# First transforms with regrouped channels and two-bank PSUM tiles, and a wider second inverse transform, in a convolution and two-expert-layer kernel

## The chip, the cores and the metric

The kernel runs on 1 core of one Trainium2 chip. The metric is the device time of one execution in microseconds (us). Before the change the median of 3 runs is 1278.2 us (1269.12 to 1280.97). A measurement of this kernel can tell about 1% from no change.

## The reference, cut to what matters

Three layers follow one another. `x` is (4, 5696, 128), `h` is (5696, 128); every number is fp32.

```python
# 1: long convolution along the sequence, channel by channel
Xf = np.fft.rfft(x, n=2*S, axis=1); Hf = np.fft.rfft(h, n=2*S, axis=0)
x = np.fft.irfft(Xf * Hf[None], n=2*S, axis=1)[:, :S].reshape(B*S, D)
# 2: soft mixture of experts over 32 slots
logits = x @ phi                        # (22784, 32)
d = softmax of logits over tokens;      slot_input = d.T @ x
slot_out[e] = relu(slot_input[e] @ w1[e]) @ w2[e]
x = (softmax of logits over slots) @ slot_out
# 3: top-1 routed mixture of 8 experts
e = argmax(x @ w_gate + modality_bias[modality_id]);  out = gate * (relu(x @ w1[e]) @ w2[e])
```

The change touches how layer 1 is transformed and how the slot logits and slot inputs of layer 2 are made. Layer 3 (more than half of the time) is not touched.

## The kernel before

The convolution is done with a transform written as two matmul steps. The sequence of 5696 is split as 89 x 64 (`N1`, `N2`). The first step is a transform of length 89 over the partitions, the second one of length 64 with the twiddle factors in its matrix `G`. There are five sequences in turn: `h`, then the four batches of `x`.

**Stage 1 of each sequence (`st1`, `columns`).** The sequence lies in `xr` as 89 partitions by (channel half, s, 64 channels). For one channel of each half the stationary operand (the weights that TensorE, PE in the profile, loads before a matmul) is `x[:, :, d+i]`: 128 columns, each 64 floats (256 bytes) from the next. The moving operand is `fw1`, 180 columns of cosines and sines. A PSUM tile `psa` of one bank takes two such matmuls. (An fp32 matmul is two instructions in the trace, each with its weight load, so a sequence has 64 matmuls and 128 instructions.) A tile is emptied into `A` by four copies of 64 lanes x 180 elements: two on ScalarE (ACT), lanes 0 to 63 (L124), two on VectorE (DVE), lanes 64 to 127 (L126). The framework orders any two instructions of different engines that touch the same PSUM bank, so the DVE copies of a tile wait for its ACT copies. Four tiles are in rotation (`psa`, bufs=4), a tag that `psy` and `psl2` share later.

**Steps of each sequence (`X`, `YT`, `PH`, `YL`).** 23 steps of four frequencies. `X` multiplies `A` (weights 2 floats apart) with `G`; for `x` DVE multiplies the result with the spectrum of `h` into U and V (L192, L193), GpSimd (POOL) adds and subtracts them into Y (L195, L196). Three steps later `YT` turns Y and ACT copies it out (L206) for a store, `PH` projects it on phi (`psl`, L216, copied by ACT, L220), and `YL` turns the projection (`psl2`, copied by ACT, L235). During the steps SyncE's queue (SP) loads the next sequence, in eight pieces of two DMAs. The last steps of a sequence run among the first of the next. Small jobs (`w2split_jobs`) that split a weight matrix, one ACT cast (L300) and one DVE subtraction (L301) each, are taken one after each group of four `psa` tiles.

**`slot_logits`.** `psi` (L368): the first inverse step on the projected spectrum, 128 lanes in and 89 out, copied into `A2` by ACT and DVE in turn. `psb` (L390): the second inverse step, 16 groups of 16 instructions, contracting over 89 lanes, with weights from `c_iv2` (`Bt`, four tiles in rotation, two DMAs each, loaded three groups ahead). Each `psb` group is copied by ACT into `L` (L405), then by DVE (L397), which also takes maxima (L399). After the last group a chain of small DVE and PE instructions makes the column maximum `cm`.

**`slot_inputs`.** `less` subtracts `cm` (DVE, then POOL), `weights` takes the exponential on ACT (L503), and `columns` transforms the weights `L` with the same `fw1` into `AW` (`psw`, contiguous weights, 32 tiles of one bank, 4 in rotation); now and then the DVE takes one of ACT's copies (`swap`). Transform, dot with the stored spectra and so on follow.

Everything here is in `tc.manual_schedule()`: each engine runs its instructions in the order of the program, and SP its DMAs. `yr.load()` issues the load of one 512 KB piece of the stored spectra into a ring of 19 slots that lie in `xr`, `ring`, `a2` and `Lf`. PE runs short warm-up matmuls (`keep_warm`) at a few places.

Of the kernel before, what the change touches and what calls it, by code (L numbers as in the profile page):

```python
# [12 lines left out]
F32 = mybir.dt.float32  # L13
# [8 lines left out]
B, S, D = 4, 5696, 128  # L22
# [32 lines left out]
def shape_constants():  # L55
# [54 lines left out]
NB = (N1 + 3) // 4  # L110
NPAIR = (N1 + 1) // 2


def columns(nc, ps, xs, fw1, n, put, swap=False, view=lambda v: v):

    m = len(xs)
    f = fw1.rearrange("p (r k) -> p r k", r=2)[:, :, :n]
    for i, x in enumerate(xs):
        nc.tensor.matmul(ps[:, i], x, f, start=True, stop=True)  # L119
    for j in range(2):  # L120
        for r in range(2):
            o, v = put(r, j), view(ps[64 * j:64 * j + 64, :m, r])
            if j == 0 and not (swap and r):
                nc.scalar.copy(o, v)  # L124
            else:
                nc.vector.tensor_copy(o, v)  # L126


def conv_spectra(nc, tc, I, R, P, jobs, xr, ahead):

    G, ident, phi, fw1 = P["G"], P["ident"], P["phi"], P["fw1"]
    with tc.tile_pool(name="p1", bufs=1) as sp, tc.tile_pool(name="p1p", bufs=2, space=PS) as pp:
        H = sp.tile([128, N1, 128], F32, name="H")
        A = sp.tile([128, NPAIR, D, 2], F32, name="A")
        seqs = [("h", 0)] + [("x", b) for b in range(B)]
        xt = xr.rearrange("p (h s d) -> p h s d", h=2, d=64)[:N1]
        nc.gpsimd.memset(xr[64:], 0.0)

        def load(q, c):

            if q < len(seqs):
                src = I["x"][seqs[q][1]].rearrange("(p s) (h d) -> p h s d", s=N2, h=2)
                h, s = divmod(c, 4)
                dma89(nc.sync, xt[:, h, 16 * s:16 * s + 16], src[:, h, 16 * s:16 * s + 16])

        def load_h():

            src = I["h"].rearrange("(p s) d -> p s d", s=N2)
            t = A.rearrange("p k d e -> p (k d e)")[:N1, :N2 * D].rearrange("p (s d) -> p s d", d=D)
            for c in range(0, N2, 16):  # L150
                dma89(nc.sync, t[:, c:c + 16], src[:, c:c + 16])
            for c in range(0, N2, 16):
                for h in range(2):
                    o, v = xt[:, h, c:c + 16], t[:, c:c + 16, 64 * h:64 * h + 64]
                    if h == 0:
                        nc.scalar.copy(o, v)  # L156
                    else:
                        nc.vector.tensor_copy(o, v)

        def st1(c):  # L160

            for d in range(8 * c, 8 * c + 8, 2):
                ps = pp.tile([128, 2, 2, 2 * NPAIR], F32, name="psa", tag="psa", bufs=4)
                x = xr.rearrange("p (m d) -> p m d", d=64)
                columns(nc, ps, [x[:, :, d + i] for i in range(2)], fw1, 2 * NPAIR,
                        lambda r, j: A[64 * r:64 * r + 64, :, 64 * j + d:64 * j + d + 2].rearrange("p k d e -> p d k e"),
                        view=lambda v: v.rearrange("p i (k e) -> p i k e", e=2))

        load_h()
        keep_warm(nc, pp, P["ones"], NWARM, tag="psa", bufs=4)  # L170

        class Seq:
# [4 lines left out]
            def X(self, i):  # L177
# [4 lines left out]
                if self.kind == "h":  # L182
# [4 lines left out]
                    return  # L187
                U = sp.tile([128, 4, 2, 64], F32, name="U", tag="U", bufs=2)
                V = sp.tile([128, 4, 2, 64], F32, name="V", tag="V", bufs=2)
# [3 lines left out]
                nc.vector.tensor_tensor(V[:, :n], psv[:, :n], h[:, :, 1:2, :].to_broadcast([128, n, 2, 64]), op=ALU.mult)  # L193
                y = sp.tile([128, 4, 2, 64], F32, name="Y", tag="Y", bufs=LAG + 3)
                nc.gpsimd.tensor_tensor(y[:, :n, 0], U[:, :n, 0], V[:, :n, 1], op=ALU.subtract)  # L195
# [3 lines left out]
            def YT(self, i):  # L199
                n = nk4(i)  # L200
                y = self.Y[i]
                ps = pp.tile([128, 4, 128], F32, name="psy", tag="psa", bufs=4)
                for m in range(n):
                    turned(nc, ps[:, m, :], y[:, m].rearrange("p r c -> p (r c)"), ident)
                yt = sp.tile([128, 4, 128], F32, name="yt", tag="yt", bufs=3)
                nc.scalar.copy(yt[:, :n], ps[:, :n])  # L206
                nc.sync.dma_start(R["yt"][:, self.b, 4 * i:4 * i + n, :], yt[:, :n])

            def PH(self, g):

                ps = pp.tile([128, 2, 128], F32, name="psl", tag="psl", bufs=1)
                n = min(8, N1 - 8 * g)
# [12 lines left out]
            def YL(self, g):  # L225
# [4 lines left out]
                o = self.o[:, 8 * (g % 2):8 * (g % 2) + n]  # L230
                ps = pp.tile([128, 2, 128], F32, name="psl2", tag="psa", bufs=4)
                if n == 8:
# [28 lines left out]
        for q in range(len(seqs)):  # L261
            z = Seq(q)
            for c in range(8):
                st1(c)
                if q > 0 and jobs and c < 7:
                    jobs.pop(0)(sp)
                if q == 0 and c < 6:
                    P["loadG"](c)
            for i in range(NB):
                for _ in range(2 if i == 0 else 1):  # L270
                    if tail:
                        tail.pop(0)()
                z.step(i)
                if q > 0 and i == 18 and jobs:
                    jobs.pop(0)(sp)
                if i % 2 == 0 and i < 16:
                    load(q + 1, i // 2)
# [62 lines left out]
def slot_logits(nc, tc, I, R, P, a2, xr, yr, Lf):  # L340

    ident, ones, iv1 = P["ident"], P["ones"], P["iv1"]
    L = Lf.rearrange("p (j s) -> p j s", s=N2)
    A2 = a2[:N1].rearrange("p (x j) -> p x j", x=128)
    yls = [t[:, YLW * i:YLW * i + YLW] for t in (xr, Lf) for i in range(2)]
    with tc.tile_pool(name="p2", bufs=1, reuse_waits="tile") as sp, tc.tile_pool(name="p2p", bufs=3, space=PS, reuse_waits="tile") as pp:
        Bt = {}
        BC = 4

        def load_yl(b):  # L350
            nc.sync.dma_start(yls[b], R["ylt"][b].rearrange("p k s -> p (k s)"))

        def load_B(c):
            if c < N2 // BC:
                t = sp.tile([N1, BC, 2, N1], F32, name="Bt", tag="Bt", bufs=4)
                dma89(nc.sync, t, I["c_iv2"][:, BC * c:BC * c + BC])
                Bt[c] = t
        nc.gpsimd.memset(Lf[64:, 2 * YLW:], 0.0)
        load_yl(2)
        load_yl(3)  # L360
        for _ in range(4):
            yr.load()
        for b in range(B):
            yl = yls[b].rearrange("p (k s) -> p k s", s=NS)
            for s in range(0, NS, 4):
                ps = pp.tile([N1, 4, 128], F32, name="psi", tag="a")
                for j in range(4):
                    nc.tensor.matmul(ps[:, j], yl[:, :, s + j], iv1, start=True, stop=True)  # L368
                o = A2[:, :, b * NS + s:b * NS + s + 4].rearrange("p x j -> p j x")
                if s % 8 == 0:  # L370
                    nc.scalar.copy(o, ps)
                else:
                    nc.vector.tensor_copy(o, ps)
            for _ in range((2, 4, 0, 0)[b]):
                yr.load()
            if b < 3:
                load_B(b)
        SC = 8
# [3 lines left out]
        for s in range(0, N2, 4):  # L382
            c = s // SC
            if s % SC == 0:
                st = sp.tile([N1, B, SC, NS], F32, name="lst", tag="lst", bufs=2)
            ps = pp.tile([N1, 4, B, NS], F32, name="psb", tag="a")
# [25 lines left out]
        keep_warm(nc, pp, ones, W1, tag="w", bufs=1)  # L412
        pt = pp.tile([NS, N1], F32, name="pt", tag="a")
        turned(nc, pt, m1, ident[:N1, :N1])
# [5 lines left out]
        keep_warm(nc, pp, ones, W2, tag="w", bufs=1)  # L420
        pb = pp.tile([N1, NS], F32, name="pb", tag="a")
        nc.tensor.matmul(pb, ones[:NS, :N1], dg, start=True, stop=True)
# [55 lines left out]
def slot_inputs(nc, tc, I, R, P, a2, yr, L, cm, c, prefetch, cT):  # L478

    G, fw1 = P["G"], P["fw1"]  # L480
    with tc.tile_pool(name="p3p", bufs=2, space=PS, reuse_waits="tile") as pp:
# [30 lines left out]
        weights(8, JC)  # L512
        for j in range(0, 128, 4):
            ps = pp.tile([128, 2, 2, N1 + 1], F32, name="psw", tag="a", bufs=4)
            columns(nc, ps, [L[:, j + i:j + i + 2].rearrange("p j s -> p (j s)") for i in (0, 2)], fw1, N1 + 1,
                    lambda r, i: AW[64 * r:64 * r + 64, :, j + i:j + i + 3:2].rearrange("p k j e -> p j k e"), j % 16 == 4,
                    view=lambda v: v.rearrange("p i (k e) -> p i k e", e=2))
            if j % 8 == 0 and j + JC < 128:
                weights(j + JC, j + JC + 8)
            if j % JC == JC - 4:  # L520
                yr.load()
# [22 lines left out]
        for i in range(NB + 1):  # L544
# [6 lines left out]
            if i >= 12:  # L551
                cT.make(pp, tag="a", bufs=4)
        prefetch()
# [884 lines left out]
```

## Time and profile before

| what | us |
|---|---|
| median of 3 runs | 1278.2 |
| the profiled execution, its own time | 1284.36 |
| its span, first to last instruction | 1282.5 |
| PE busy in the span | 985.3 |
| DVE busy | 680.9 |
| ACT busy | 607.8 |
| POOL busy | 527.0 |

[...] The convolution runs to about 360 us, `slot_logits` to about 454 us, `slot_inputs` to about 544 us; the rest is the experts, the routing and the routed experts. A line of the trace names the engine, the line of the kernel, the operation, the tiles (written tile, arrow, read tiles) and shapes; "idle before" is the engine's idle time ahead of the instruction and what ended it.

### The profile page before, as it was taken

The page shows a single profiled execution, that of the slowest core. Times are in us where ns is not written, and L with a number is a line of the kernel's source. Part 1 is how long each engine was busy: PE and PEld are TensorE (multiplying, and loading weights), DVE is VectorE, ACT ScalarE, POOL GpSimd, SP SyncE. Part 2 cuts the span into 40 slices and gives each one's busy share as a digit, 9 for nine tenths or more (in the row PEclk, how much of TensorE's full clock was granted, in tenths as well). Part 3 has the DMA queues.
Part 4 walks back from the last instruction along what each step waited for, and adds up shares of the span by engine and source line. Part 5 has one row for each costly group of instructions (what it writes and reads, how often), then busy time and mean ns, then how long its engine had stood idle before and what let it go on. Part 6 is the DMA issues. An engine that isn't in the chain of part 4 may idle for free.

```text
span 1282.5 us, 23978 instructions
## 1 busy us (share of the span) xinstructions
PE 985.3 (77%) x7670; PEld 907.4 (71%) x7670; DVE 680.9 (53%) x1421; ACT 607.8 (47%) x1519; POOL 527.0 (41%) x603
## 2 busy tenths in 40 slices
PE   7999999999999988983229723540018999999996
PEld 7998988889899966843129623540017999999996
DVE  3577777868734589353008512430005666666664
ACT  4464655657444272221008511420006777777775
POOL 2006345270720045126740357267663444444443
PEclk8999999999999599986559856775558999999999
DMA  9538576583785468974210000001011111111112
GB/s 281 78 73 202 169 186 204 155 249 121 245 294 145 113 221 258 359 240 135 68 45 14 13 13 15 10 21 34 28 33 37 38 38 39 38 38 40 36 40 76
DMA packets 151600, 142.45 MB, mean 111 GB/s; under 512 B 72156, under 2 KB 126876, under 8 KB 150348
## 3 DMA queue, kind: packets, MB, share of 16 engines
q1 hardware_dynamic: 139752, 125.04, 33.6%
q0 software_dynamic: 11456, 14.79, 3.9%
q8 instruction: 64, 1.05, 0.4%
q10 hardware_dynamic: 264, 1.05, 0.2%
q14 instruction: 64, 0.52, 0.1%
HBM read 218.45 MB, written 57.77 MB: 215 GB/s over the span
## 4 chain that ended last, share of the span: by engine, by line
PE 66%; another core or an unknown queue 12%; issue 9%; DVE 7%; ACT 4%; DMA 2%; POOL 0%; SPq 0%; ACTq 0%; POOLq 0%; DVEq 0%
PE psa L119 11%; PE ph L1091 9%; PE psx L181 9%; PE acc L1105 5%; PE acc L1104 5%; PE acc L1106 5%; PE psb L390 3%; PE psi L368 3%; PE psy L93 3%; PE pso L93 3%; PE psl L216 2%; ACT yT L1110 2%; DVE A L126 2%; PE psS L540 1%
## 5 line engine op out<-in xcount | busy, mean ns | idle before, releaser
L1094 DVE SCALAR_TENSOR_TENSOR hl<-ph,hh 128x512 fp32r<-128x512 f32 x360 | 247.9, 691 | 249.1 <-ACT hh L1093 125.0
L1129 POOL DMA_INDIRECT out<-y,rt x180 | 174.9, 972 | 222.0 <-ACT y L1118 175.8
L1093 ACT ACTIVATE hh<-ph 128x512 fp32r<-128x512 f32 x360 | 216.1, 602 | 99.8 <-PE ph L1091 48.5
L1091 PE MATMUL ph<-x,wm 128*128 128x256 f32 x720 | 164.1, 312 | 104.5 <-ACT x L1082 65.0
L1001 POOL DMA_INDIRECT s_rec<-rec,posi x178 | 173.3, 974 | 134.1 <-issue 53.6
L1105 PE MATMUL acc<-hl,wo 128*128 128x256 f32 x720 | 208.0, 289 | 5.0 <-issue 5.0
L1104 PE MATMUL acc<-hh,wo 128*128 128x256 f32 x720 | 208.2, 289 | 1.5 <-issue 1.5
L1106 PE MATMUL acc<-hh,wo 128*128 128x256 f32 x720 | 207.8, 289 | 1.8 <-issue 1.8
L1091 PEld LDWEIGHTS ph<-x,wm 128*128 128x128 f32 x720 | 114.5, 199 | 106.9 <-ACT x L1082 66.9
L195 POOL TENSOR_TENSOR Y<-U,V 128x256 f32<-128x256 f32 (+1 forms) x92 | 65.4, 711 | 222.5 <-DVE V L193 222.0
L119 PE MATMUL psa<-fw,xr 128*128 128x180 f32 x640 | 143.0, 386 | 6.8 <-ACT xr L156 6.8
L119 PEld LDWEIGHTS psa<-fw,xr 128*128 128x128 f32 x640 | 142.0, 313 | 8.2 <-issue 8.2
L1105 PEld LDWEIGHTS acc<-hl,wo 128*128 128x128 f32 x720 | 142.5, 198 | 5.3 <-issue 5.1
L1106 PEld LDWEIGHTS acc<-hh,wo 128*128 128x128 f32 x720 | 142.4, 198 | 1.7 <-issue 1.7
L1104 PEld LDWEIGHTS acc<-hh,wo 128*128 128x128 f32 x720 | 142.3, 198 | 1.2 <-issue 1.2
L181 PE MATMUL psx<-G,A 128*128 128x128 f32 x890 | 125.9, 289 | 3.0 <-DVE A L126 1.5
L181 PEld LDWEIGHTS psx<-G,A 128*128 128x128 f32 x890 | 113.3, 199 | 20.2 <-DVE U L192 12.4
L126 DVE COPY A<-psa 64x180 f32<-64x180 f32 x320 | 111.6, 349 | 28.4 <-ACT A L124 20.0
L124 ACT COPY A<-psa 64x180 f32<-64x180 f32 x320 | 98.2, 307 | 37.0 <-PE psa L119 34.5
L93 PE MATMUL pso<-ident,yT 128*128 128x128 f32 x180 | 39.9, 305 | 72.7 <-issue 58.6
L206 ACT COPY yt<-psy 128x512 f32<-128x512 f32 (+1 forms) x92 | 52.6, 572 | 83.1 <-PE psy L93 65.4
L1082 ACT CAST x<-pst 128x256 fp32r<-128x256 f32 x90 | 33.6, 373 | 115.1 <-PE pst L93 59.0
(197 smaller groups left out, 1420.5 us busy)
## 6 DMA issues: line engine op xcount, KB each, us to landing
wo<-s_wsc SPq DMA_DIRECT2D x90, 1024.0 KB
wm<-s_mwsc SPq DMA_DIRECT2D x180, 256.0 KB
s_yt<-yt SPq DMA_DIRECT2D x88, 256.0 KB
xr<-x SPq DMA_DIRECT2D x32, 320.0 KB
xr<-s_yt SPq DMA_DIRECT2D x20, 512.0 KB
s_wsc<-ws SPq DMA_DIRECT2D x32, 256.0 KB
L<-s_yt SPq DMA_DIRECT2D x16, 512.0 KB
s_ylt<-ylt SPq DMA_DIRECT2D x20, 256.0 KB
```

The lines of the kernel that those rows point to most:

```text
L93: nc.tensor.transpose(out, in_, ident)
L119: nc.tensor.matmul(ps[:, i], x, f, start=True, stop=True)
L126: nc.vector.tensor_copy(o, v)
L181: nc.tensor.matmul(ps[:, m, :], A[:, 2 * i + m // 2, :, m % 2], G[:, 4 * i + m, :], start=True, stop=True)
L1001: i = nc.gpsimd.indirect_dma_start(R["rec"], bass.IndirectOffsetOnAxis(ap=posi[:, g:g + 1], axis=0), rec[:, g, :], None, bounds_check=SPAR ...
L1091: nc.tensor.matmul(ps[:, TM * j:TM * j + TM], wm[k % 3][:, 128 * f:128 * f + 128], x[k], start=True, stop=True)
L1093: nc.scalar.activation(o, ps, AF.Relu)
L1094: nc.vector.scalar_tensor_tensor(hl[:, 2 * q:2 * q + 2].rearrange("p j t -> p (j t)"), ps, 0.0, o.bitcast(F32), op0=ALU.max, op1=ALU.subtract)
L1104: nc.tensor.matmul(acc[k], wh, hh[:, f], start=(f == 0), stop=False)
L1105: nc.tensor.matmul(acc[k], wh, hl[:, f], start=False, stop=False)
L1106: nc.tensor.matmul(acc[k], wl, hh[:, f], start=False, stop=(f == 7))
L1129: i = nc.gpsimd.indirect_dma_start(out, bass.IndirectOffsetOnAxis(ap=r[:, j, NS + 1:RW].bitcast(I32), axis=0), y[:, j, :], None, bounds_ch ...
```

## The change

- The sequence is loaded into `xr` as (s, 128 channels), in four pieces of two DMAs, `h` too (which came through `A` before, copied into `xr` by ACT and DVE).
- `spread(c)` copies four channel pairs at a time, 89 lanes x 512 elements, into one of three small tiles `xs`, where the weights of a matmul are 2 floats (8 bytes) apart. POOL does it three tiles ahead; for the first three tiles of a batch ACT does it in the steps 17, 19 and 21 of the sequence before.
- `columns` now takes a PSUM tile of two banks with four matmuls, two tiles in rotation. The four copies are of 64 lanes x 360 elements, and the ACT copies and the DVE copies of one tile are declared free of each other. `psw` uses the same function, in 16 tiles.
- `psl` and `psl2` become two halves of one PSUM bank that is allocated once; U and Y become one tile in 5 buffers.
- `psb` contracts over 128 lanes: `c_iv2` has zero rows, `A2` gets zeros by four POOL memsets (lanes 96 to 127) and by the `psi` copies (lanes 89 to 95, from three PSUM tiles that DVE clears first). `Bt` chunks 0 to 3 are loaded at the start into four tiles, 4 to 11 into `xr` after the second batch of `psi`, 12 to 15 as the tiles come free, with one DMA each. Six `yr.load()` move from the `psi` stage to the groups 12 to 14 of `psb`.

```diff
+NXS = 3
+def columns(nc, tc, pp, xs, fw1, put, swap=False, **k):
+    ps = pp.tile([128, 4, 256], F32, **k)
+    pv = ps[:, :, :4 * NPAIR].rearrange("p i (r k e) -> p r i k e", r=2, e=2)
     for i, x in enumerate(xs):
-        nc.tensor.matmul(ps[:, i], x, f, start=True, stop=True)
+        nc.tensor.matmul(ps[:, i, :4 * NPAIR], x, fw1, start=True, stop=True)
     for j in range(2):
         for r in range(2):
-            o, v = put(r, j), view(ps[64 * j:64 * j + 64, :m, r])
+            o, v = put(r, j), pv[64 * j:64 * j + 64, r]
             if j == 0 and not (swap and r):
-                nc.scalar.copy(o, v)
+                i = nc.scalar.copy(o, v)
+                tc.declare_no_dep(i.ins, group="half1", ...)
+                tc.add_to_no_dep_group("half0", i.ins)
...
+        xs = [sp.tile([128, 2, 128, 2], F32, name=f"xs{i}") for i in range(NXS)]
+        xv = xr.rearrange("p (s h q e) -> p q h s e", h=2, q=32, e=2)[:N1]
+        def spread(c, eng=None):
+            o, v = xs[c % NXS][:N1].rearrange("p q (h s) e -> p q h s e", h=2), xv[:, 2 * c:2 * c + 2]
+            if eng is nc.scalar:
+                nc.scalar.copy(o, v)
+            else:
+                nc.gpsimd.tensor_copy(o, v)
...
-            for c in range(8):
+            if q == 0:
+                for c in range(NXS):
+                    spread(c)
+            for c in range(16):
                 st1(c)
+                if c + NXS < 16:
+                    spread(c + NXS)
-                if q > 0 and jobs and c < 7:
+                if q > 0 and jobs and c % 2 and c < 14:
                     jobs.pop(0)(sp)
...
+        for x in range(0, 16 * F, 4 * F):
+            nc.gpsimd.memset(a2[96:, x:x + 4 * F], 0.0)
+        pst = [pp.tile([128, 4, 128], F32, name=f"psi{i}", tag=f"a{i}", bufs=1) for i in range(3)]
+        for t in pst:
+            nc.vector.memset(t[64:], 0.0)
...
-            load_B(s // BC + 3)
+            if s // BC < NBT:
+                load_B(s // BC + N2 // BC - NBT)
+            if s // BC >= N2 // BC - NBT and s // BC < N2 // BC - NBT + 3:
+                yr.load()
+                yr.load()
```

## Rows read from the trace of the kernel before

**Rows 1.** Page, part 4: chain that ended last, shares by line.
```profile
PE psa L119 11%; PE ph L1091 9%; PE psx L181 9%; PE acc L1105 5%; PE acc L1104 5%; PE acc L1106 5%; PE psb L390 3%; PE psi L368 3%; PE psy L93 3%; PE pso L93 3%; PE psl L216 2%; ACT yT L1110 2%; DVE A L126 2%; PE psS L540 1%
```
**Rows 2.** Windows: length, busy (count) of PE, PEld, DVE, ACT, POOL; clock; DMA, GB/s.
```profile
19.10:48.60 29.50, 29.43 (x128) 29.23 (x128) 21.14 (x61) 19.02 (x62) 0.00 (x0) 0.93 0.41 167
60.00:72.00 12.00, 12.00 (x104) 12.00 (x104) 4.47 (x7) 3.53 (x7) 0.00 (x0) 1.00 0.77 118
142.10:170.50 28.40, 28.40 (x134) 28.39 (x131) 23.49 (x68) 21.73 (x71) 1.69 (x4) 1.00 0.37 112
360.50:400.40 39.90, 39.90 (x257) 39.79 (x256) 15.59 (x16) 17.09 (x19) 2.17 (x1) 1.00 0.77 247
401.60:410.60 9.00, 8.94 (x80) 8.75 (x80) 5.68 (x7) 4.22 (x4) 0.00 (x0) 1.00 0.36 94
...
412.30:449.80 37.50, 37.50 (x177) 37.50 (x178) 18.95 (x23) 10.20 (x10) 0.00 (x0) 0.50 0.43 116
459.40:484.20 24.80, 22.96 (x120) 18.07 (x120) 22.84 (x66) 23.24 (x68) 8.53 (x6) 1.00 0.79 266
```
**Rows 3.** Groups by line: busy us, mean ns of one, idle before and its releasers.
```profile
L119 PE MATMUL psa<-fw,xr 128*128 128x180 f32 x640 | 143.0, 386 | 6.8 <-ACT xr L156 6.8
L119 PEld LDWEIGHTS psa<-fw,xr 128*128 128x128 f32 x640 | 142.0, 313 | 8.2 <-issue 8.2
...
L119 PEld LDWEIGHTS psw<-fw,L 128*128 128x128 f32 x128 | 19.3, 189 | 9.9 <-ACT L L503 6.9
```
**Rows 4.** Groups by line, the copies of PSUM tiles and the job on DVE.
```profile
L126 DVE COPY A<-psa 64x180 f32<-64x180 f32 x320 | 111.6, 349 | 28.4 <-ACT A L124 20.0
L124 ACT COPY A<-psa 64x180 f32<-64x180 f32 x320 | 98.2, 307 | 37.0 <-PE psa L119 34.5
...
L301 DVE TENSOR_TENSOR ws<-wa,ws 128x256 fp32r<-128x256 f32 x32 | 14.9, 467 | 7.1 <-ACT ws L300 6.3
...
L503 ACT ACTIVATE L<-L 89x512 f32<-89x512 f32 (+1 forms) x17 | 10.3, 605 | 6.6 <-DVE L L499 6.3
...
L186 DVE COPY H<-psx 128x512 f32<-128x512 f32 (+1 forms) x12 | 7.9, 658 | 15.3 <-PE psx L181 15.3
...
L184 ACT COPY H<-psx 128x512 f32<-128x512 f32 x11 | 6.4, 585 | 17.5 <-PE psx L181 17.5
```
**Rows 5.** Groups by line, POOL.
```profile
L195 POOL TENSOR_TENSOR Y<-U,V 128x256 f32<-128x256 f32 (+1 forms) x92 | 65.4, 711 | 222.5 <-DVE V L193 222.0
...
L137 POOL MEMSET xr<- 64x8192 f32 x1 | 6.9, 6923 | 0.1
...
L1336 POOL CAST identr<-ident 128x128 fp32r<-128x128 f32 x1 | 0.3, 283 | 0.0
```
**Rows 6.** Timeline, first ACT instructions: start, us, engine, line, operation, idle before.
```profile
7.18 1.28 ACT L156 ACT_TABLE_LOAD   x1 [7.18 <-DMA A<-h]
...
18.02 1.05 ACT L156 COPY xr<-A 89x1024 f32<-89x1024 f32 x1 [2.67 <-DMA A<-h]
```
**Rows 7.** Timeline of the steps, one `ylt` copy and the `psl` matmuls after it.
```profile
122.55 0.38 ACT L235 COPY ylt<-psl 128x256 f32<-128x256 f32 x1
...
123.52 0.64 PE L216 MATMUL psl<-Y,phi 128*32 128x256 f32 x8
```
**Rows 8.** Timeline, from the last job through `psi` to `psb`.
```profile
360.54 20.09 PE L368 MATMUL psi<-iv,xr 128*89 128x128 f32 x128
361.18 0.43 DVE L301 TENSOR_TENSOR ws<-wa,ws 128x256 fp32r<-128x256 f32 x1 [4.56 <-ACT ws L300]
...
412.25 37.54 PE L390 MATMUL psb<-A,Bt 89*89 89x128 f32 x176 [1.67 <-DMA Bt<-c_iv]
```
**Rows 9.** Timeline of DVE at the end of `psb`.
```profile
445.72 0.84 DVE L409 TENSOR_REDUCE m<-mx 89x32 f32<-89x416 f32 x1
447.48 0.69 DVE L397 COPY lst<-psb 89x512 f32<-89x512 f32 x1 [0.91 <-ACT L L405]
448.20 1.02 DVE L399 TENSOR_REDUCE mx<-lst 89x32 f32<-89x512 f32 x1
```

More of the change, by code (lines that the diff above doesn't have):

```diff
@@ L72, in shape_constants @@
     iv2 = np.stack([np.cos(ps), np.sin(ps)], 2) / S
+    iv2 = np.concatenate([iv2, np.zeros((128 - N1,) + iv2.shape[1:])])
     sel = np.tile(np.eye(NS), (B, 1))
@@ L160, in st1 @@
-        def st1(c):
[L162 to L167, printed above, removed]
@@ L169, in conv_spectra @@
-        load_h()
-        keep_warm(nc, pp, P["ones"], NWARM, tag="psa", bufs=4)
+                kind, b = seqs[q]
+                src = (I["x"][b] if kind == "x" else I["h"]).rearrange("(p s) d -> p s d", s=N2)
+                dma89(nc.sync, xt[:, 16 * c:16 * c + 16], src[:, 16 * c:16 * c + 16])
+        def st1(c):
+            x, d = xs[c % NXS], 4 * c
+            columns(nc, tc, pp, [x[:, i // 2, :, i % 2] for i in range(4)], fw1,
+                    lambda r, j: A[64 * r:64 * r + 64, :, 64 * j + d:64 * j + d + 4].rearrange("p k d e -> p d k e"),
+                    name="psa", tag="psa", bufs=2)
@@ L172, in conv_spectra @@
+        for c in range(4):
+            load(0, c)
+        keep_warm(nc, pp, P["ones"], NWARM, tag="psa", bufs=2)
+        pl = pp.tile([128, 4, 128], F32, name="psl", tag="psl", bufs=1)
         class Seq:
@@ L201, in YT @@
                 y = self.Y[i]
-                ps = pp.tile([128, 4, 128], F32, name="psy", tag="psa", bufs=4)
+                ps = pp.tile([128, 4, 128], F32, name="psy", tag="psa", bufs=2)
                 for m in range(n):
@@ L209, in PH @@
             def PH(self, g):
-                ps = pp.tile([128, 2, 128], F32, name="psl", tag="psl", bufs=1)
+                ps = pl[:, :2]
                 n = min(8, N1 - 8 * g)
@@ L230, in YL @@
                 o = self.o[:, 8 * (g % 2):8 * (g % 2) + n]
-                ps = pp.tile([128, 2, 128], F32, name="psl2", tag="psa", bufs=4)
+                ps = pl[:, 2:]
                 if n == 8:
@@ L275, in conv_spectra @@
                     jobs.pop(0)(sp)
-                if i % 2 == 0 and i < 16:
-                    load(q + 1, i // 2)
+                if i % 4 == 0 and i < 16:
+                    load(q + 1, i // 4)
+                if q + 1 < len(seqs) and i % 2 and i >= NB - 2 * NXS:
+                    spread((i - NB) // 2 + NXS, nc.scalar)
                 if q == B and i % 2 == 0 and 2 <= i < 18:
@@ L348, in slot_logits @@
         BC = 4
+        NBT = 4
         def load_yl(b):
@@ L360, in slot_logits @@
         load_yl(3)
+        for c in range(NBT):
+            load_B(c)
         for _ in range(4):
             yr.load()
+        for x in range(0, 16 * F, 4 * F):
[3 more added lines that the diff above has]
+            nc.vector.memset(t[64:], 0.0)
         for b in range(B):
@@ L365, in slot_logits @@
             for s in range(0, NS, 4):
-                ps = pp.tile([N1, 4, 128], F32, name="psi", tag="a")
+                ps = pst[(b * NS + s) // 4 % 3]
                 for j in range(4):
-                    nc.tensor.matmul(ps[:, j], yl[:, :, s + j], iv1, start=True, stop=True)
-                o = A2[:, :, b * NS + s:b * NS + s + 4].rearrange("p x j -> p j x")
+                    nc.tensor.matmul(ps[:N1, j], yl[:, :, s + j], iv1, start=True, stop=True)
+                o = A2[:96, :, b * NS + s:b * NS + s + 4].rearrange("p x j -> p j x")
                 if s % 8 == 0:
-                    nc.scalar.copy(o, ps)
+                    nc.scalar.copy(o, ps[:96])
                 else:
[L373 to L377, printed above, removed]
+                    nc.vector.tensor_copy(o, ps[:96])
+            if b == 1:
+                for c in range(NBT, N2 // BC - NBT):
+                    load_B(c)
         SC = 8
@@ L385, in slot_logits @@
                 st = sp.tile([N1, B, SC, NS], F32, name="lst", tag="lst", bufs=2)
-            ps = pp.tile([N1, 4, B, NS], F32, name="psb", tag="a")
+            ps = pp.tile([N1, 4, B, NS], F32, name="psb", tag=f"a{s // 4 % 3}", bufs=1)
             for j in range(4):
@@ L512, in slot_inputs @@
         weights(8, JC)
[L513 to L518, printed above, removed]
+        for j in range(0, 128, 8):
+            columns(nc, tc, pp, [L[:, j + i:j + i + 2].rearrange("p j s -> p (j s)") for i in (0, 2, 4, 6)], fw1,
+                    lambda r, i: AW[64 * r:64 * r + 64, :, j + i:j + i + 7:2].rearrange("p k j e -> p j k e"), j % 24 == 8,
+                    name="psw", tag="a", bufs=2)
+            if j + JC < 128:
                 weights(j + JC, j + JC + 8)
-            if j % JC == JC - 4:
+            if j % JC == JC - 8:
                 yr.load()
```

52 lines of the change are left out of this document (21 added, 31 removed).

## The prediction, made before the result was known

> **What bounds the kernel now.** I read the chain of waits first, by line: PE holds most of it, and three of its lines are the ones that the change works on, `psa` (11%), `psi` and `psb` (3% each) [rows 1]. So each of these stages has to be opened to see whether PE is held up by its own rate or by a partner.
>
> The windows of the stages say that. In stage 1 of a batch PE is busy for all of 28.40 us at clock 1.00, while DVE and ACT have 5 to 7 us to spare [rows 2]. Its 128 instructions are thus spaced by 28.4/128 = 222 ns. The reader should set beside this two other stages at clock 1.00: `psx`, with weights 8 bytes apart, has 104 instructions in 12.00 us (115 ns for 128 moving columns), and `psb`, with contiguous weights, 80 in 8.94 us (112 ns) [rows 2]. If time went with the columns, 180 of them would take 112 x 180/128 = 157 ns. The missing 65 ns are in the weight load: 313 ns for `psa`, whose columns lie 256 bytes apart, and 189 ns for `psw`, which has the same shape and contiguous columns [rows 3]. In stage 1 PEld is as full as PE [rows 2]: the strided weight load is the bound.
>
> `psb` has two halves. The first 9.00 us run at clock 1.00. [...] `psi`, with 128 lanes in and the same 89 out, keeps 1.00 over 39.90 us [rows 2]. In `psw` no engine is full: PE 22.96, DVE 22.84 and ACT 23.24 of 24.80 us [rows 2]; tiles wait for their copies.
>
> **Stage 1, matmuls.** With weights 8 bytes apart I take 157 ns an instruction; nothing in the trace says that 180 columns behind such a load cost more. A tile of four matmuls (eight instructions) then takes 8 x 157 = 1.26 us, and the 128 instructions of a sequence 20.1 us.
>
> **Stage 1, copies.** 64 lanes x 360 elements are not in the trace. On DVE they cost at least one old copy, 349 ns, and at most two, 698; the line through 180 elements (349) and 512 (658) gives 349 + 180/332 x 309 = 517, and I take 0.52. On ACT the same line through 307 and 585 gives 0.46 [rows 4]. Two copies a tile are 1.04 us on DVE and 0.92 on ACT, now side by side. With two tiles in rotation, tile n+2 starts when tile n is empty: seven spacings of 157 and the last matmul's 386 ns [rows 3] are 1.48 us, the copies 1.04, and I allow 0.15 for the hand-overs. That is 2.67 us for two tiles, 1.33 each, a little over PE's own 1.26: 16 x 1.33 = 21.4 us. In seven of eight pairs of a batch a job adds 0.47 on DVE [rows 4] and up to 0.4 of waiting for its ACT cast, behind which DVE's next copies queue, and PE behind these: 2 x 1.04 + 0.47 + 0.25 = 2.8 a pair, 7 x 2.8 + 2.67 = 22.3 us. Four batches: 4 x (22.3 - 28.4) = -24.4. For `h` (29.50 now) the opening runs at the low clock in both kernels (0.93 on average [rows 2]); the old matmuls were weight-bound and lost 1.0 there, the new ones lose about 2: 23.5, so -6.0. **Stage 1 in all: -30.4.** Its ends: PE alone (20.1 each), -40.5; copies of 0.70 us, where DVE is the bound with (4 x 0.70 + 0.47 + 0.4)/2 = 1.83 a tile, 29.3 us a batch, +1.
>
> **Stage 1, the spread.** A POOL copy of 512 elements costs at least 0.43 us at the memset's rate (6.92 us for 8192) and at most 1.42 at that of the two-input subtraction (711 ns for 256); by the one-input cast (283 ns for 128) it is 1.13 [rows 5], and I take 1.0. POOL has 1.69 us of work in stage 1 today [rows 2], and a tile takes 1.33, so 13 or 16 spreads hide under the matmuls; without that cover, each us of a spread over 1.33 costs 13 us a batch. For `h` the first spread replaces the last ACT copy ahead of the first matmul at 19.1 us: nothing. ACT's table load, which stands before its first copy at 7.18 us [rows 6], moves to the first `psa` copy: 0 to +1.3, taken as +0.8. The three ACT spreads of a batch cost between 0.58 (512 elements [rows 4]) and about 1.0 us, off PE's path unless `ylt` waits for them.
>
> **Steps.** In the shared bank the `psl` matmuls now wait for the `ylt` copy of the other half. That copy ends at 122.93, they start at 123.52 [rows 7]: 0.59 us of slack, which an ACT spread just before it can eat. With the shorter rotation of `psy` at the seams: 0 to +5, taken as **+1.5**. The DMAs of the loads halve in number and stay off the path.
>
> **`psi`.** Its rate stays. The three PSUM clears stand on DVE behind the last job, which ends at 361.61, while `psi` starts at 360.54 [rows 8]: with about 0.5 for the first clear, **+1.6** (0 to +2.5). The `A2` zeros are four POOL memsets of 4096 columns, 3.46 us each by the row of 8192 [rows 5], 13.8 in all, and follow POOL's clear of `L` in this 40 us window; `psb` needs them at its end. `Bt` chunks 4 to 11 (2.9 MB) are issued when half of `psi` is done, 20 us ahead of `psb`, in a window that moves 247 GB/s [rows 2]: under 12 us, so the wait of 1.67 goes. The six spectrum loads moved into `psb` (3 MB) lie ahead of the softmax loads on SP; `psw` covers these.
>
> **`psb`.** 256 x 112 ns = 28.7 us against 48.2 (401.6 to 449.8 [rows 2]): -19.5. DVE is late next: a group costs it 0.69 + 1.02 = 1.71 us and PE 1.79, so it keeps up, but runs 1 us behind ACT's copy, and the extra maximum of 0.84 [rows 9] is no longer hidden in an idle gap: about +1.8 before the last maximum. **-17.7.** Lower bound -19.5; upper in the rivals.
>
> **`psw`.** For 15 tiles of eight columns now 24.8 us. Halving the copies gives ACT 25 x 0.46 + 11 x 0.605 = 18.2 and DVE 35 x 0.52 = 18.2; PE needs 18.9, the rotation 15 x 1.33 = 20.0. In a swapped tile DVE still waits for ACT. I take 22.3: **-2.5** (-5 to 0).
>
> **Sum.** -30.4 + 0.8 + 1.5 + 1.6 - 17.7 - 2.5 = -46.7. The profiled execution took 1284.4 us (span 1282.5 and 1.9 around it) and would take 1237.7; it stood 6.2 above the median of the runs, so the median becomes 1278.2 - 46.7 = **1231.5 us**.
>
> **Rivals.** (a) *POOL's spread becomes the bound, and the kernel is slower.* At T us a spread, a batch's stage 1 takes about 1.5 + 13T + 1.4 and that of `h` 1.4 + 16T. At T = 2.5 that is 35.4 and 41.4, +28 and +12 against now, so -46.7 + 30.4 + 40 = +24: 1302 us. It turns slower from T = 2.2 on. For it: no row has POOL reading in 8-byte pieces. Against: the highest row gives 1.42. 4%.
> [...]
> (b) *The clock stays at 0.50 in `psb`* though 128 lanes work: all 256 instructions at 213 ns are 54.5 us, 26 more than forecast: 1257. Against: `psi` at 1.00 with the same 89 columns. 5%.
> (c) *The two engines don't empty a tile at once*, because an order remains in the program or the chip makes one wait: (1.48 + 0.92 + 1.04 + 0.15)/2 = 1.8 a tile, 28.7 a batch, and `psw` as before: -46.7 + 30.4 + 1 + 2.5 = -12.8: 1265. 4%.
> (d) *The layout of the weights does not matter*: 222 ns stay, -46.7 + 30.4 = -16.3: 1262. The rows against it are 313 and 189 ns for the same 128 columns [rows 3]. 2%.
> [...]
> (e) *Copies are cheaper than the line, and PE is the bound*: up to 10 less, 1221. 8%.
> (f) *Copies cost 0.70*: stage 1 gains nothing: 1263. 4%.
>
> **Chances.** The forecast's own case has 73%, with 1216 to 1248 from the ends of its terms. The range 1215 to 1250 takes in (e) and leaves out the others. About 1% (12.8 us) is what a measurement can tell from no change, so faster means under 1265.4: forecast, (b), (d), (e), (f) and most of (c), 0.92; within 1%: 0.04; slower: (a), 0.04.
>
> **What would show it.** `psa` spaced by about 157 ns with a load near 190; DVE copies near 0.52 starting together with ACT's; POOL spreads of 1 us; stage 1 of 22 us; `psb` at clock 1.00 in 29 us without a DMA wait; `psi` 1.6 later. A stage 1 over 27 us, or a clock of 0.50 in `psb`, would prove me wrong.

## The result, and the profile after

The changed kernel takes **1240.26 us** (median of 4 runs, 1238.53 to 1246.82) against 1273.66 for the kernel before beside it (median of 4, 1267.15 to 1280.97): ratio 0.9721, 95% interval 0.968 to 0.9763. Faster, and inside the range, 8.8 us above the forecast of 1231.5. The profiled execution took 1240.95 us (span 1239.1).

The chain by line, part 4 of the page of the changed kernel, answers to [rows 1]:

```profile
PE ph L1117 10%; PE psx L188 9%; PE acc L1132 6%; PE acc L1131 6%; PE acc L1130 6%; PE psa L122 5%; PE psi L392 3%; PE psy L94 3%; PE pso L94 3%; DVE A L133 2%; PE psl L222 2%; ACT yT L1136 2%; PE psb L413 2%; PE psS L566 1%
```

`psa` fell from 11 to 5% and `psb` from 3 to 2%. The windows show what became of the stages; columns as in [rows 2] (length; busy and count of PE, PEld, DVE, ACT, POOL; granted clock of TensorE, 1.00 being its full speed; DMA share, GB/s). In order: `h`, the second batch, `psi`, `psb`, the start of `psw` and the rest of it.

```profile
18.60:42.80 24.20, 23.50 (x128) 21.41 (x128) 16.98 (x31) 16.83 (x31) 9.46 (x15) 0.92 0.63 234
...
130.80:154.30 23.50, 21.55 (x132) 19.59 (x128) 18.85 (x37) 18.90 (x39) 9.85 (x16) 1.00 0.40 121
...
336.70:376.90 40.20, 40.15 (x256) 39.86 (x256) 16.55 (x18) 16.75 (x18) 12.70 (x4) 1.00 0.68 245
378.20:406.30 28.10, 28.06 (x257) 28.09 (x258) 24.40 (x29) 15.92 (x15) 0.00 (x0) 1.00 0.56 152
411.40:419.40 8.00, 6.53 (x32) 5.70 (x32) 6.29 (x7) 3.83 (x8) 7.83 (x4) 0.79 0.71 224
419.40:444.90 25.50, 19.12 (x110) 16.35 (x108) 18.33 (x35) 18.42 (x37) 6.11 (x5) 1.00 0.82 280
```

Beside [rows 2]: a batch of stage 1 takes 23.1 us instead of 28.4, and PE has idle time in it, so the weight load is no longer the bound; `psb` runs in one piece at clock 1.00 (28.1 us for the 46.5 of its two parts there, and no wait between). The groups by line (busy us, mean ns of one, idle before and its releasers), against [rows 3, 4]:

```profile
L122 PE MATMUL psa<-fw,xs 128*128 128x180 f32 x640 | 109.7, 325 | 14.5 <-POOL xs L157 7.7 <-DVE A L133 4.5 <-ACT A L127 0.2
L122 PEld LDWEIGHTS psa<-fw,xs 128*128 128x128 f32 x640 | 99.8, 199 | 24.5 <-POOL xs L157 15.3 <-issue 7.6 <-ACT A L127 1.4
L133 DVE COPY A<-psa 64x360 f32<-64x360 f32 x160 | 88.3, 552 | 36.6 <-PE psa L122 32.2
L127 ACT COPY A<-psa 64x360 f32<-64x360 f32 x160 | 83.6, 522 | 41.2 <-PE psa L122 37.2 <-ACT A L127 0.3
...
L157 POOL COPY xs<-xr 89x512 f32<-89x512 f32 x68 | 45.8, 675 | 93.8 <-PE psa L122 73.3 <-DMA xr<-h 15.0 <-ACT ws L313 2.8
```

The load fell from 313 to 199 ns. The copies cost 552 and 522 ns where 517 and 460 were forecast. POOL's copy costs 675, not 1000, and waits for PE.

Stage by stage, each start read from the two profiled executions (first matmul of the stage; `cm` is the start of the subtraction behind the column maximum):

| term | forecast | measured | how |
|---|---|---|---|
| stage 1 with the table load | -29.6 | -26.3 | `h` starts 0.56 earlier and takes 24.10 instead of 29.43 (23.5 forecast); batches 23.81, 23.14, 23.13, 23.15 instead of 28.32 and three of 28.42 |
| steps, shared bank, seams | +1.5 | +2.4 | `psi` starts at 336.72 instead of 360.54: -23.8 so far |
| `psi` and its clears | +1.6 | +0.4 | `psb` starts at 378.24 instead of 401.64: -23.4 |
| `psb` to `cm` | -17.7 | -19.0 | `cm` at 411.47 instead of 453.89: -42.4 |
| `psw` | -2.5 | +0.7 | `px` at 445.0 instead of 486.7: -41.7 |
| behind `px` | 0 | -1.7 | spans 1239.1 and 1282.5: -43.4 |

A later comparison of the same two kernels gave 1005.0 us (1002.79 to 1006.63, 6 runs) and 1043.81 us (1036.37 to 1048.21, 11 runs), ratio 0.9637 (0.9602 to 0.9673). There the stages up to `px` have the same lengths (`px` at 445.0 again), and the routed experts behind them take 400 us from the first `ph` to the last instead of 600, in all kernels. The changed kernel comes to its first `ph` at 573 us instead of 625. The difference is idle time and not work: PE is busy 895.8 us of the shorter span (1002.3) and 928.9 of the longer one (1239.1). What it waits for there was not studied. So totals below are compared within one comparison only, the stages across all.

### The profile page after: what moved, and what is told of

Read it like the earlier page. It is cut to its first block, busy times and chain, and to the rows that moved or that the text cites. A ratio compares the mean times of both kernels' runs of the same rounds, so it can differ in the third digit from the quotient of the medians.

```text
span 1239.1 us, 23518 instructions
## 1 busy us (share of the span) xinstructions
PE 928.9 (75%) x7670; PEld 844.4 (68%) x7670; DVE 650.9 (53%) x1225; ACT 594.5 (48%) x1338; POOL 581.2 (47%) x677
## 4 chain that ended last, share of the span: by engine, by line
PE 60%; issue 12%; another core or an unknown queue 10%; DVE 8%; ACT 5%; DMA 3%; SPq 1%; POOL 0%; ACTq 0%; POOLq 0%; DVEq 0%
PE ph L1117 10%; PE psx L188 9%; PE acc L1132 6%; PE acc L1131 6%; PE acc L1130 6%; PE psa L122 5%; PE psi L392 3%; PE psy L94 3%; PE pso L94 3%; DVE A L133 2%; PE psl L222 2%; ACT yT L1136 2%; PE psb L413 2%; PE psS L566 1%
## 5 line engine op out<-in xcount | busy, mean ns | idle before, releaser
L122 PE MATMUL psa<-fw,xs 128*128 128x180 f32 x640 | 109.7, 325 | 14.5 <-POOL xs L157 7.7
L122 PEld LDWEIGHTS psa<-fw,xs 128*128 128x128 f32 x640 | 99.8, 199 | 24.5 <-POOL xs L157 15.3
L133 DVE COPY A<-psa 64x360 f32<-64x360 f32 x160 | 88.3, 552 | 36.6 <-PE psa L122 32.2
L127 ACT COPY A<-psa 64x360 f32<-64x360 f32 x160 | 83.6, 522 | 41.2 <-PE psa L122 37.2
L201 POOL TENSOR_TENSOR Y<-Y,V 128x256 f32<-128x256 f32 (+1 forms) x92 | 65.6, 713 | 63.6 <-DVE V L200 57.6
```

The lines of the kernel that those rows point to most:

```text
L122: nc.tensor.matmul(ps[:, i, :4 * NPAIR], x, fw1, start=True, stop=True)
L133: i = nc.vector.tensor_copy(o, v)
```

## The experiments

**Is the spread of the kernel before in the stages that the change touches?** The kernel before, unchanged.

> The kernel before, unchanged, profiled a second time. Its runs so far lie in two pairs, 1267 and 1269, 1278 and 1281 us, and the profiled one was of the upper pair; profile against profile the change gave 43.4 us, median against median 33.4. Theory A: the 11 us lie in the convolution and slot stages that the change touches (the clock in psb falls later or not at all in the lower pair): then psb takes clearly under 48.2 us in a profile of about 1269 us, and the change is worth less against such a run. Theory B: they lie behind slot_inputs, in the routing, whose waits the change does not touch: then psb is 48 us again, px starts at 486.7 us again, and the difference comes later.

Measured: 1272.94 us (1264.03 to 1278.57, 10 runs), ratio 0.9986 (0.9949 to 1.0023). Its profiled execution, 1278.57, is the slowest of its ten, and still has `psb` at 48.4 us and `px` at 486.1. So two profiled executions of it that lie 5.8 us apart differ by 0.5 up to `px`: that much of the spread lies behind these stages, as theory B has it. Theory A spoke of the executions near 1269 us, and none of those was profiled.

**Is it the layout of the weights?** Everything new, but the weights come straight from `xr`, 256 bytes apart, with the old loads (and so without `spread`). One run of each of this kernel and the next two stands beside a median of 1271.16 us for the kernel before:

```diff
-            x, d = xs[c % NXS], 4 * c
-            columns(nc, tc, pp, [x[:, i // 2, :, i % 2] for i in range(4)], fw1,
+            x, d = xr.rearrange("p (m d) -> p m d", d=64), 4 * c
+            columns(nc, tc, pp, [x[:, :, d + i] for i in range(4)], fw1,
...
```

> The kernel after with one part undone: stage 1 takes its weights straight from xr, 256 bytes apart, in the old loads (no spread); two-bank tiles and copies by two engines at once stay. Mine (the strided weight load is the bound): 222 ns an instruction, weight load 313 ns, stage 1 of a batch 28.4 us again, some 1260 to 1265 us in all. Rival (the two-bank tiles and the freed copies gave the gain): stage 1 stays at 23 to 24 us, 1240 us in all.

Measured: 1259.03 us; a batch takes 28.6 to 28.8 us, as before the change. Groups by line of that kernel:

```profile
L122 PEld LDWEIGHTS psa<-fw,xr 128*128 128x128 f32 x640 | 142.7, 313 | 8.6 <-issue 7.9
```

The load is back at 313 ns, and two-bank tiles alone bring nothing: PE is held by its loads again. Rival (d) falls.

**Is it the tile?** Spread weights, but one-bank tiles, four in rotation, with the framework's order of the copies, in stage 1 (`columns1` is `columns` of the kernel before); `psw` keeps the new tile:

```diff
+            for u in range(2):
+                ps = pp.tile([128, 2, 2, 2 * NPAIR], F32, name="psa", tag="psa", bufs=4)
...
+                columns1(nc, ps, [x[:, u, :, i] for i in range(2)], fw1, 2 * NPAIR, ...)
```

> The kernel after with the other part undone: spread weights stay, but stage 1 has its old one-bank tiles of two matmuls, four in rotation, with DVE's copies ordered behind ACT's; psw keeps the new form. Mine: the matmuls could take 19 to 20 us a batch, but DVE needs 64 copies of 0.35 us and seven jobs of 0.43, 25.5 us with nothing between them, so stage 1 takes 26 to 28 us a batch. Rival (the layout alone gives all): 20 to 22 us.

Measured: 1255.23 us; batches of 25.7 and 26.0 us. The layout alone is thus worth 2.4 us a batch, and the tiles 2.9 more on top of it, though without it they are worth nothing: once the load is short, the small tiles with their ordered copies hold the stage next.

**Must the two engines empty a tile at once?** The new kernel without the declaration that the copies are free of each other:

```diff
-                tc.declare_no_dep(i.ins, group="half1", ...)
-                tc.add_to_no_dep_group("half0", i.ins)
...
-                tc.declare_no_dep(i.ins, group="half0", ...)
-                tc.add_to_no_dep_group("half1", i.ins)
```

> The kernel after, where DVE's copies of a two-bank tile stay ordered behind ACT's, in psa and psw; all else as in the kernel after. Mine: two tiles take 1.48 for the matmuls, two ACT copies of 0.52, two DVE copies of 0.55 and 0.15, that is 1.9 us a tile, 30 us a batch in stage 1, slower than the kernel before there (28.4). Rival (the chip makes one engine wait for the other anyway, or copies get shorter when they run alone): 23 to 25 us.

Measured: 1275.01 us; batches of 28.75 us, 1.80 a tile, which is what rival (c) put on this case and less than the 30 us expected here, because a copy alone is cheaper than was taken. With the copies in order, large tiles are slower than small ones (26.0). Groups by line of that kernel:

```profile
L131 DVE COPY A<-psa 64x360 f32<-64x360 f32 x160 | 85.7, 535 | 78.7 <-ACT A L127 74.6
L127 ACT COPY A<-psa 64x360 f32<-64x360 f32 x160 | 74.3, 464 | 79.8 <-PE psa L122 78.6
```

DVE waits for ACT 74.6 us in all. The rows also give the price of a copy that has the tile to itself: 464 and 535 ns, against a mean of 522 and 552 where the two may run at once. Emptying a tile from two sides is worth 5.6 us a batch all the same. Two things about the higher price are in the traces. In this kernel, too, copies of the two engines overlap in time, ACT's on the next tile, and those cost no more: from 150.75 us on two of ACT's take 0.92 us while DVE is busy all through, and 79 of DVE's lie between 534 and 539 ns. And in the changed kernel the price goes with the start: where ACT and DVE begin on a tile within 50 ns of each other (93 of 160 pairs in stage 1) the copies cost 556 and 561 ns in the median, where ACT is 0.3 us or more ahead on the same tile (47 pairs) 468 and 536, as alone.

**Why does `psb` keep its clock: the wider contraction, or the missing wait?** Three kernels, one execution of each, take the two apart: 89 lanes and no late load; 128 lanes and one late `Bt` chunk (issued behind the fourth group, needed by the sixth); 89 lanes and the late chunk. The 89 lanes take `w[:N1]` and `A2[:N1]` instead of `w` and `A2`; the late chunk is:

```diff
-                    load_B(c)
+                    if c != NBT + 1:
+                        load_B(c)
...
+                if s // BC == NBT - 1:
+                    load_B(NBT + 1)
```

> The kernel after, but the psb matmuls contract over lanes 0 to 88 only, as before; loads, zeros and everything else as in the kernel after, so no Bt load is late. It tells apart why the clock fell in psb. Wait theory (the 1.67 us gap let it fall, and without a gap it holds): psb 28 us at clock 1.00, 1240 us in all. Lanes theory (89 lanes by 89 columns cannot hold the full clock): it falls some 9 us into psb, without a gap, and the rest runs at 213 ns an instruction: psb 45 to 48 us, 1258 to 1260 us in all.

> The kernel after with one Bt chunk (number 5) loaded late, so that psb waits once for a DMA, some 2 us, as the kernel before did; 128 lanes. Lanes theory: the clock stays at 1.00 or falls for a few us and comes back while psb runs, psb 30 to 33 us. Wait theory (a gap alone decides, and the rest of the stage stays at the low clock whatever the lanes): psb about 48 us.

> The late Bt chunk and the contraction over 89 lanes together, in the kernel after: the conditions of the kernel before. Both theories: the clock falls after the gap and does not come back in psb, 46 to 49 us. If it does come back, neither holds and something else of the kernel before kept it low.

Measured: 1003.76, 1012.61 and 1027.66 us, beside 1045.8 for the kernel before; `psb` takes 28.15, 34.09 and 51.20 us. The windows over `psb`, first of the 89 lanes without a late load:

```profile
378.20:406.30 28.10, 28.10 (x257) 28.10 (x258) 24.45 (x29) 15.91 (x15) 0.00 (x0) 1.00 0.55 155
```

Then of 128 lanes with the late chunk: its wait in the timeline (start, length, instruction, idle before and releaser), and the windows ahead of and behind it:

```profile
391.19 14.10 PE L414 MATMUL psb<-A,xr 128*89 128x128 f32 x112 [4.06 <-DMA xr<-c_iv]
```

```profile
378.20:387.10 8.90, 8.90 (x80) 8.71 (x80) 5.63 (x7) 4.22 (x4) 0.00 (x0) 1.00 0.55 138
391.20:395.00 3.80, 3.80 (x20) 3.80 (x21) 0.00 (x0) 0.17 (x1) 0.00 (x0) 0.55 0.03 9
395.00:405.10 10.10, 10.10 (x95) 10.10 (x94) 9.02 (x11) 6.19 (x6) 0.00 (x0) 1.00 0.35 90
```

And of 89 lanes with the late chunk:

```profile
392.92 24.16 PE L414 MATMUL psb<-A,xr 89*89 89x128 f32 x112 [4.44 <-DMA xr<-c_iv]
```

```profile
379.50:388.40 8.90, 8.86 (x80) 8.75 (x80) 5.59 (x7) 4.21 (x4) 0.00 (x0) 1.00 0.56 139
392.90:417.00 24.10, 24.08 (x113) 24.10 (x114) 10.26 (x12) 6.12 (x6) 0.00 (x0) 0.50 0.18 47
416.90:430.50 13.60, 13.60 (x65) 13.60 (x65) 7.61 (x9) 4.11 (x4) 0.00 (x0) 0.50 0.79 246
```

The waits came out at 4 us where some 2 were meant, so `psb` is longer than expected in the last two kernels. The reader sees three things. Without a wait, 89 lanes hold a granted clock of 1.00 over 28.10 us as well as 128 do. After a wait of 4 us both run at a lower one, 0.55 in the mean of the first 3.80 us over 128 lanes and 0.50 over 89. From there 128 lanes are back at 1.00 after 3.8 us, while 89 lanes stay at 0.50 to the end, 37.7 us, as in the kernel before (37.5 us) [rows 2, 8]. So in this change the removed wait alone gives the 20 us of `psb`'s matmuls; the 128 lanes would have been worth something only had a wait remained (17 us behind one of 4 us, 34.09 against 51.20).

**What holds the copies?** POOL does the jobs' subtraction instead of DVE, and no copy of `psw` is swapped to DVE:

```diff
-                nc.vector.tensor_tensor(w[:, 1], a, w[:, 0].bitcast(F32), op=ALU.subtract)
+                nc.gpsimd.tensor_tensor(w[:, 1], a, w[:, 0].bitcast(F32), op=ALU.subtract)
...
-                    lambda r, i: AW[...], j % 24 == 8,
+                    lambda r, i: AW[...], False,
```

> A version that should beat both: the subtraction of the small weight-splitting jobs runs on POOL instead of DVE, and no ACT copy of psw is swapped to DVE. In the kernel after, two tiles of stage 1 without a job take 2.75 us and four with two jobs 5.87; DVE waits 0.45 for the job's ACT cast and then works 0.43. Mine: without that, stage 1 of a batch goes from 23.2 to about 21.8 us (4 batches: -5.5), and psw from 1.79 to 1.57 us a tile (the swapped copy waits for ACT; ACT's 0.94 + 0.63 is the bound then), -3: 1231 to 1234 us. Rival: the cast on ACT holds the tiles as much as DVE's part did, and ACT is as late in psw: 1238 to 1241.

Measured: 997.48 us (996.93 to 1000.5, 4 runs) against 1045.8, ratio 0.9544 (0.9494 to 0.9594); batches of 22.3 to 22.6 us, `psw` 28.5 instead of 30.5, `px` at 439.9 instead of 445.0. That is 5 of the 8.5 us expected (batches of 21.8, `psw` 3 shorter): between the theory and its rival. As the better kernel it was timed again beside the changed one:

> The changed kernel as it is, for a comparison on one chip with the next two. Theory: the change is worth what its stages gained up to px, 41.7 us, and the experts behind it run as before; so the medians should stand 40 to 43 us apart where both kernels have enough runs, and px starts at 445.0. Rival: part of the gain is given back behind the stages that were changed (the 33.4 us between the first medians), then the medians stand some 33 us apart again though px starts at 445.0.

> The changed kernel with the subtraction of the weight-split jobs on GpSimd instead of VectorE and without the swapped copies in psw (that is pool_job_no_swap once more). Theory: what the copies of the two-bank tiles wait for is worth 5 us: px starts at 440 and the median is 4 to 6 us under that of the changed kernel on the same chip. Rival: the later stages swallow it, or the difference between the two chips was the cause, and the medians are within 2 us.

Measured: 1005.0 us for the changed kernel (above) and 1000.0 (997.23 to 1001.23, 6 runs; ratio to the kernel before 0.958, 0.9544 to 0.9616) for this one, whose runs all lie below; `px` starts at 445.0 and 439.1. The runs of the second experiment bear out its theory. What the jobs did in stage 1 stands in the timeline of the changed kernel:

```profile
140.61 0.41 ACT L313 CAST ws<-wa 128x256 fp32r<-128x256 f32 x1
...
141.03 0.95 ACT L127 COPY A<-psa 64x360 f32<-64x360 f32 x2
141.05 0.43 DVE L314 TENSOR_TENSOR ws<-wa,ws 128x256 fp32r<-128x256 f32 x1 [0.45 <-ACT ws L313]
...
141.39 2.20 DVE L133 COPY A<-psa 64x360 f32<-64x360 f32 x4
...
142.61 4.56 PE L122 MATMUL psa<-fw,xs 128*128 128x180 f32 x26 [0.40 <-DVE A L133]
...
144.11 2.34 ACT L127 COPY A<-psa 64x360 f32<-64x360 f32 x4 [0.50 <-PE psa L122]
144.12 2.36 DVE L133 COPY A<-psa 64x360 f32<-64x360 f32 x4
```

DVE waits 0.45 us for ACT's cast, its copies start 0.36 behind ACT's, and PE waits 0.40 for them. The last two lines are a pair without a job: the copies start together and each takes longer (2.34 us for four of ACT's, against 0.95 for two above). On the medians: the theory of the first of these two experiments put 40 to 43 us between the kernel before and the changed one, its rival 33; 38.8 were measured, nearer to the theory and outside it.

**Does the shared `psl` bank cost the steps?** As the last kernel, and `psl2` moves into the second bank of the `psy` tile:

```diff
+            def two(self):
+                self.t2 = pp.tile([128, 2, 4, 128], F32, name="psy", tag="psa", bufs=2)
...
-                ps = pl[:, 2:]
+                if self.t2 is None:
+                    self.two()
+                ps = self.t2[:, 1]
```

> As best_again, and psl2 leaves the bank that it shares with psl: it takes the second bank of the two-bank tile of psy (allocated by YL and used by YT of the same step). Theory: the shared bank costs PE one wait of 0.6 us a batch (psl behind the ylt copy), so psi starts 1.5 to 2.5 us earlier than in best_again (333.0) and the median falls by as much. Rival: psl2 now waits for a psy tile to be copied out, and the steps get longer by 1 us a batch or more; psi starts at 335 or later.

Measured: 1010.67 us (1009.16 to 1012.33, 6 runs), 10.7 above the kernel without this; `psi` starts at 344. The rival was right, and stronger than put. PE waits 8.6 us in 14 places for `psy` behind `ylt` copies, where the kernel without this waits 2.5 us for `psl`. The longest one in the timeline:

```profile
129.07 0.64 ACT L155 COPY xs<-xr 89x512 f32<-89x512 f32 x1
...
129.62 0.36 ACT L249 COPY ylt<-psy 128x256 f32<-128x256 f32 x1
...
130.12 0.63 PE L94 MATMUL psy<-ident,Y 128*128 128x128 f32 x4 [1.16 <-ACT ylt L249]
```

`psy` now stands behind the `ylt` copy, which ACT runs after a spread here. In the changed kernel at the same place it was `psl` that waited, for 0.63 us. So the shared bank is the cheaper place; a layout without either wait was not found.

**Does the clock after `psb`'s wait come back in some executions?** The 89 lanes with the late chunk, timed:

> late_chunk_89 once more, timed: the changed kernel with psb over 89 lanes and one Bt chunk late; everything ahead of psb and behind it is as in the changed kernel, whose six runs on one chip lay between 1002.79 and 1006.63 us at mean clocks of 0.964 to 0.971, while eleven runs of the kernel before there lay between 1036.37 and 1048.21 at 0.942 to 0.965, the slower ones at the lower clocks. Theory: the spread of the kernel before is psb: after the wait the clock comes back in some executions and not in others. Then this kernel spreads as the kernel before does, by 10 us or more, from about 1010 to 1028, at mean clocks about 0.02 apart, and its median lies under the 1027.66 of the profiled execution. Rival: the spread lies in the stages behind psb, which this kernel has in common with the changed one: then its runs lie within 5 us of each other, near 1027.

Measured: 1027.89 us (1025.33 to 1032.23, 6 runs), `psb` 51.3 us, mean clocks 0.942 to 0.946. The theory fell: with a wait of 4.56 us none of the six executions got its clock back, as far as their mean clocks tell (one was profiled). They spread by 6.9 us, more than the 5 of the rival. The runs of the kernel before beside it lay between 1031.61 at a mean clock of 0.971 and 1046.8 at 0.950.

## Why the prediction came out as it did

**The layout of the weights: right.** 313 ns became 199, and with the old spacing they are 313 again. Within a tile the instructions start 152 to 153 ns apart, where 157 was taken; in the second batch only the first two of a tile can stand further apart, up to 264. So rival (d) falls here too: the two traces have 313 and 199 ns for the same 128 columns.

**The copies of a two-bank tile: the mechanism right, the term mis-sized.** The straight line through two sizes gave 0.52 and 0.46 us, and a copy that has the tile to itself does cost 535 and 464 ns. The step that failed is to let both engines read the tile at once at the price of one alone: at once they cost 552 and 522 in the mean, and 561 and 556 where they start together. With the forecast's own hand-overs two tiles take 1.48 + 2 x 0.561 + 0.15 = 2.75 us instead of 2.67; with the jobs' subtraction on POOL they do take 22.4/8 = 2.80. The jobs were priced about right: off DVE they give 0.7 us a batch back, and the forecast had put 7 x 0.13 = 0.9 on them. So a batch takes 23.1 us instead of 22.3. The first one takes 23.8: a job's subtraction takes 0.81 us there instead of 0.43, and PE waits 0.87 once.

**The spread: off the path, as forecast, and cheaper.** 675 ns against 1.0 us taken. The trace puts two of PE's waits down to POOL, 7.7 us in all. One is that for the first tile of `h`, 6.82 us, where PE waited 6.84 for ACT's copy before [rows 3]. The other is the 0.87 us of the first batch, and there the spread that ends last is for a tile two further on, while DVE's copies of the tile two before end only 0.15 us ahead of PE: by these times the wait is the job's. The table load cost nothing instead of 0.8: it waited for the DMA of `h` before [rows 6], and now runs ahead of all of PE's work.

```profile
0.76 1.28 ACT L127 ACT_TABLE_LOAD   x1 [0.76 <-PEq L1454]
```

**Steps: +2.4 for +1.5.** The wait at the shared bank came where it was put, about once a batch:

```profile
L222 PE MATMUL psl<-Y,phi 128*32 128x256 f32 x360 | 29.7, 389 | 2.3 <-ACT ylt L241 1.9 <-ACT yl L226 0.3
```

The seams add the wait of the first `psy` for DVE's last copies of a batch (0.4 to 0.8 us). The sum hides a piece of luck: the steps of the four batches take 4.1 us longer, and those of `h` 1.7 less, where the granted clock was 0.93 in the execution before and 1.00 in this one.

**`psi`: +0.4 for +1.6.** The first of the three clears did not stand behind the last job: DVE was idle and ran it 1.8 us ahead of `psi`, and the subtraction of that job only at 337.06.

```profile
334.89 0.48 DVE L386 MEMSET psi<- 64x512 f32 x1 [3.38 <-ACT yt L212]
```

**`psb`: right in time, half right in cause.** The wait of 1.67 us [rows 8] went, and the granted clock stayed at 1.00 for 28.15 us (28.7 taken). That DVE would end behind PE was right: the last matmul ends at 406.4, the last column maximum 2.4 us later, and PE has a gap of 2.23 us there. The third line is the warm-up that follows.

```profile
408.15 0.68 DVE L431 TENSOR_REDUCE mx<-psb 89x32 f32<-89x512 f32 x1
...
409.51 0.24 PE L94 MATMUL pt<-ident,m 89*32 89x89 f32 x1 [2.23 <-DVE m L438]
...
411.14 2.29 PE L101 MATMUL warm<-ones 128*128 128x128 f32 x10
```

What the forecast did not tell apart is which of the two parts does it: against rival (b), whose 213 ns an instruction are those of `psb` at 0.50 before (37.54 us for 176 [rows 8]), it argued from `psi`, with its 128 lanes, and the runs show that the lanes decide nothing where there is no wait.

**`psw`: +0.7 for -2.5.** Two parts of the step failed. From its first matmul to `px` the stage takes 31.8 us as before: in a swapped tile DVE's extra copy (L131) waits for ACT and holds the rotation of two, and PE waits for DVE's copies 3.3 us in all.

```profile
L122 PE MATMUL psw<-fw,L 128*128 128x180 f32 x128 | 23.4, 332 | 7.1 <-ACT L L530 3.8 <-DVE A L133 3.3
...
L131 DVE COPY A<-psw 64x360 f32<-64x360 f32 x5 | 2.6, 527 | 5.6 <-ACT A L127 5.6
```

Without the swap it takes 29.9, so this was most of the 2.5. And the start slipped by 0.7 behind `cm`: the ten warm-up matmuls ahead of `psw` take 2.29 us at a mean granted clock of 0.57, where they took 1.38 at 1.00 before. The gap of 2.23 us in PE's work came just ahead; before, PE had no such gap there.

**From the profile to the median.** By its own sum the forecast put the profiled execution at 1237.7; it took 1240.95. These 3.3 us are the terms above (+5.0 up to `px`) less 1.7 that came behind it, most of it in `px` itself (53.6 us for 55.1). That they are so few is in part luck: stage 1, the steps and `psw` together came out 7.4 us worse than forecast, and `psi`, `psb` and what lies behind `px` 4.2 better. The other 5.5 come from taking the 6.2 us by which the profiled execution before stood over its median off the changed kernel as well: that one stands 0.7 over its own. The excess did not belong to both. The runs of the kernel before spread by 10 to 15 us in each comparison and those of the changed one by 4 to 8, so the spread seems to be mostly of something that the change removed; that is argued, not shown. A `psb` whose clock falls in some executions and not in others would do it, and a run at 0.971 beside others at 0.947 to 0.955 fits; but no profile shows such an execution, and the timed experiment with the longer wait never recovered. This stays open. One slip in the chances: the words put most of (c) under faster, the figures count all of it as within 1%.

## What to carry to other kernels

Compare the weight load's time with that of a like matmul with contiguous weights (here 313 ns against 189) before anything else, and then look at what the shorter load uncovers: here the layout alone gave 2.4 us a batch of the 5.3, and the larger tile gave nothing without it. Price a PSUM copy for the case in which another engine starts on the same tile at the same moment (here 556 and 561 ns against 464 and 535 alone), and keep odd jobs out of the queue of the engine that frees tiles (here 0.7 us a batch). In a stream of small matmuls, look for the one DMA wait ahead of a low clock: removing it was worth twelve times its own length here (20 us for 1.67).

## What the hardware showed that was not expected

- A stream of 89 x 89 weights holds a granted clock of 1.00 for 28 us, but once at 0.50 it stays there for at least 37.7 us without a gap; the same stream over 128 lanes was back at 1.00 after 3.8 us (one profile, as for the 28 us; two for the 37.7).
- ACT and DVE read the two halves of the lanes of one PSUM tile at 556 and 561 ns a copy (medians) where they start together, and at 468 and 536 where ACT is 0.3 us or more ahead; one after the other they take 464 and 535.
- A GpSimd copy of 89 x 512 elements in 8-byte pieces takes 630 to 675 ns, 1.2 to 1.3 ns an element, against 2.2 for the 128-element cast, one instruction, that the forecast leaned on [rows 5].
